# A new hand-placed order and new PSUM banks for a Conformer block on one core

## The chip, the cores and the metric

The kernel runs on one core of a Trainium2 chip. A core has engines that run side by side, each through its own list of instructions in order: TensorE (PE in the profile) multiplies matrices, and its weight loads (PEld) are listed apart; VectorE (DVE), ScalarE (ACT) and GpSimd (POOL) work on elements; SyncE (SP) does no arithmetic here and issues DMA transfers. Engines wait for one another through semaphores. TensorE writes its results to PSUM, a memory of banks; the other operands lie in SBUF. Full inputs and outputs lie in the chip's main memory.

The metric is the device time of one execution in microseconds (us). The profile covers one execution and gives its span, from the first to the last instruction that it shows; the execution's own time is a little longer.

## The reference

`x` is 2 sequences of 4,000 tokens with 144 features, all in bf16. Abridged:

```python
h = _layernorm(x);  h = _silu(h @ w_ff1a) @ w_ff1b          # 144 -> 576 -> 144
x = x + 0.5 * h
h = _layernorm(x);  qkv = h @ w_qkv                          # 4 heads of 36
p = _softmax((q @ k.T) * Dh ** (-0.5));  att = p @ v         # 4000 x 4000 per head
x = x + att @ w_o
h = _layernorm(x);  h = h @ w_pw1;  h = a * _sigmoid(b)      # 144 -> 2 x 144
c = sum(hp[:, i:i + T, :] * dw[i] for i in range(5))         # 5 taps along the tokens
x = x + _silu(c) @ w_pw2
h = _layernorm(x);  h = _silu(h @ w_ff2a) @ w_ff2b
x = x + 0.5 * h
return _layernorm(x)
```

The attention dominates: for 2 sequences and 4 heads, 4,000 × 4,000 scores, each with an exponential.

## The kernel before

**Tiles and stages.** The 8,000 tokens are cut into 16 chunks of 500 (numbers 0 to 15, eight to a sequence), and a chunk into 4 blocks of 125 rows. Each chunk goes through the first feed-forward, then queries, keys and values, then attention over its whole sequence, then the gated convolution, the second feed-forward and the last layernorm. The chunks' stages overlap: while one chunk is in attention, the one behind it is prepared and earlier ones are finished.

**Attention.** Keys are taken 64 at a time, 62 such tiles and one of 32 a chunk. For a tile TensorE makes the score products (`scores`, line 1770: `PS<-QT,KT`); their exponential goes to ScalarE (818 activations `PT<-PS`) or, for 190 tiles, to VectorE, which makes it from integer operations (`dve_tile`, line 1811); TensorE then multiplies it with the values (`PS<-PT,VA`, for the short tile `PS<-PT,VL`) and adds up in banks 6 and 7. All other products use banks 0 to 5.

**The rest.** In the feed-forward (`ff`, line 1240; `ff_part`, line 1258, for half a chunk) the first product is `PS<-XT,WA`, its last 64 columns are `PS<-XT,WE`, the activation gives `HT`, and the second product is `PS<-WB,HT`. While exponentials are being made, SiLU is made from tanh, which stands in the same table of functions (`TH` on ScalarE, then `HT` on VectorE); behind the last exponential ScalarE loads the table for SiLU (line 2102), and `HT` comes straight from ScalarE. The convolution is `PS<-U,DG`, products with diagonal matrices. A residual addition writes `X` on VectorE. The layernorm (`ln`, line 1109) takes statistics on VectorE (`ST`), a variance and a power on GpSimd (`RS<-RS,NHALF`), and then the normalised rows `XN` on GpSimd, or at both ends of the program on VectorE or ScalarE. For the last layernorm `store` (line 1661) writes `XN` to the output; `put` (line 1655) issues the transfer on SyncE's queue or, at the end of the program, on ScalarE's. The first and the last chunks go in two halves; the others in one.

**What sets the order.** The program is first recorded, not emitted: each call of `op` (line 177) notes an instruction and what it depends on, and a scheduler (`Sched`, line 509) picks with modelled costs which thread records next. That gives every engine a list of blocks (instructions that stay together). Then `R.reorder(ORDER)` (line 281, called on line 2115) permutes the blocks of each engine. A table, `ORDER` (line 38), has a string for each of the five engines; each character is one block's shift:

```python
codes, shift = [ALPHABET.index(c) for c in table[e]], []
...
shift.append(c - 45)
...
at[i + shift[i]] = blk
```

`P` has code 45 and leaves a block where it is; the next letters put it later, the ones before it earlier; `~` opens a longer shift of two further characters. A second table, `PLACES` (line 111), names with one digit the PSUM bank (0 to 5) of each of 1,724 tiles in the order in which they were recorded (`place`, line 257). For a new order the dependencies between tiles of one bank are made anew, `finish` (line 365) works out which semaphores each instruction waits for, and `replay` (line 409) emits each engine's list. All instructions are emitted on line 419, so the profile has them all under L419 and they are told apart by their tiles; the waits for the output's transfers at the end are on line 425.

Of the kernel before, what the change touches and what calls it, by code (L numbers as in the profile page):

```python
# [39 lines left out]
        "PPPPPPPPQOPPPPROQNPPQRPQLPPRPVPSPNIZMWOMVVL~OVKLJ~OOJJNSNLMMMNPNPKSOOJ[JZKMXNKOG]NJHEKNNNE_MMMadMJLL"  # L40
        "mTLI?LJLEMZPbJNJMGrLLLLkfJKKKKKWKNNVJMKgBJJJ[QddGGMIFKEcQKLJFKNKKNNKPUMOMWTMYVIRLLISKOLPQQRPRPJQUNPQ"
        "OQKPPPPPYOOOOYNNNOMhTNLVXLMIMOSXKILOKN`NNRRNHQOXROMQOTKOUQQQTQUS]PT[`P2ALQXDMKILMNTQLSKNRNUN_PMMNOWN"
        "]NNOOSKPRPDIOQOY__MWNNN]NHMNQCGMQJNWNORTOMRRTLTPNSOBOP^UNNQMMTLNPTLLTMNOWNOOOXNOPLOPNQQMTTNNNNRSO]OQ"
        "OPPGPNROMQQLPPQOPVOcNNNNPMTNNOM]]LNNKMNPWOPNJUOOCOOXOOYZOMKcLLWXJKKSWKHKKVJNNKNORPNPQOQOSOOVNOYZMMMM"
        "NNOMPXPKOOVQMNPVOPHPYMNOQNNPN[]^LMM]MKWKKKLJKLVLP`LN_NLNOMOQNKMRMNLPPPQOS[P[MOPISOKNQMIPRPSPLQNPWORO"
        "QQKLVOQRN[QQQQJFPPPPKQQSPRKQQLPPPQVPPQOPUUOOPNCXORRNYVSSNG[MPUZPPAOKAOMUNNPVOLTUOL]KLNRPMMSNNNNdZNQM"
        "MMNNQMSLLTYMOMSHVKUO]JJ`RKTNQKMFLNQNW[]NLPHLNQNRMNFPPPS]OOLOOPPSLNNNQOSOPN`SNOMNO_PMMNOMOOLPNPYVL^[Q"
        "LNKKFMQM[TLMOOQWNQVQMKYNRNXNO8NRMMNYOOQNN^OOOQOIOSP[OPRPZGOOPN]YMNNNO<VNNKMNOYPNOOOTQM]MVJSMMRMKSPUM"
        "HOPNSOOOSOPNTPNOOROOQVNOPNO^RPQMVOHNQNLPRPJPXOOPNPNOOPXXNNNOOOWNIOOOORUOPKOSNROTXKOW[KOKLN[RZIMOIKNN"
# [20 lines left out]
    "act": (  # L70
        "PPPPPPPPPPPPPRTNNOOPPQOPPPPPPXPNOSNNNNPPPPPPQRSOLOQZQORKRSLLOQQJPPPPQQNQOPPPPPPPPPQQQMPPPPPPPPPPPPRO"
        "OPQOPQQNPPPPPPPPPPPPPPPPPPPPPPPPPPPPPPPPPPPPPPPPPPPPPPPPPPPPPPPPPPPPPQOPRORNSNOOPPPPPPPPPQOPPPPPPPPP"
        "QOPPPPPPPPPPPQOPPPPPPPPPPPPQOPPPPPPPPPPPRPNPQOPPPPPRPNPPPPPPPPPPPPPPPPPPPPPPPPPPPPPPPPPPPPPPPPPPQOQQ"
        "NPPPPPPPPPPPPPPPPPPPPPPPPPPPPPPPPPPPPPPPPPPPPPPPPPPPPPPPPPPPPPPPPPPPPQOPPPPPPPPPPPPPPQOPPQOPPPPPPPPP"
        "PQOPPPPPPPPPPPPPPPPPPPPPPPPPPPROOPQOPPPPPPPPPPPPPPPPPPPQOPPPPQOPPPPPPPPPPPPPPPPPTOOPQQLPPPPPPPPPPPPP"
        "PPPPPQOPPQOPPPPPPPQOPPPPPPPPPPQOPPQOPPPPPQQQQLQQNPPPPPPQOPPPPPPPPPPPPPPPQOPPPQOPPPPPPPPPPPPPPPPPPPPQ"
        "OPPPPPPPTOPNOROOPPPPPPPPPPPPPPPQOPQOPPPPPPPPPPQOPPPPPPPPPPPQOPPPPPPPPPPPPPPPPQOPPPPPPPPPPQOPPPPPPPPP"
        "PPPRPNPPPPPPPPPQOPPPPPPPPPPPPPPPPPPPPPQRNOPPQQNPPPPPPPQQNPPPPPPPPPPPPPPPPPQOQOPPQOPPPPPPPPPPQOQOPPPP"
        "PPPQOQOPPPPPPPPPPPPPPPPPPPPPPPPPPPPQQNPPPPPPPPPPPPPPPPPPPPQOPPPPPPPPPPPPPPROOPPPPPPPPPPPPPPPPPPPPPQQ"
        "NPPPPQOPPPPPPPQQNPPPPPPPPPQOPPPPPPPPPPPPQOPPPPPPPPPPPPPPPPPPPPPPPPPPPPPPPPPPPPPPPPPPPPPPQOPPPPPPPPPP"  # L80
        "PPPPPPPPPPPPPPPPPPPPPPPPPPPPPPPPPQOSPNRNOQOUQNPMOPPPRORNQNPPPPPPQOROQQMPPPPPPQOPPPWORNNNOO"
    ),
# [2064 lines left out]
```

## Time and profile before

| what | value |
|---|---|
| three runs, median (lowest to highest) | 879.97 us (879.73 to 881.92) |
| the profiled execution | 880.01 us |
| its span in the profile | 878.1 us |
| instructions in the span | 27,043 |

The span and the execution's own time differ by 1.91 us, which lies around the span. In the profile's rows a group of instructions is written as engine, operation, output tile `<-` input tiles, sizes (partitions × elements, type) and a count; buffer numbers are left out, so `PS` is any PSUM tile. In a timeline the first two columns are the start and the length in us, and a bracket at the end gives the engine's idle time before and what ended it. A row of waits gives the total in us, the number and the longest.

### The profile page before, as it was taken

Reading aid. Unit: us, or ns where it says so; the run is one execution under the profiler, and the core shown is the slowest. Engines: PE = TensorE matmul, PEld = TensorE weight load, DVE = VectorE, ACT = ScalarE, POOL = GpSimd, SP = SyncE. Lnnn points to the kernel's source line nnn. Section 1 sums busy time; section 2 is a strip of 40 time slices with the busy share of each in tenths; the row PEclk is TensorE's granted clock in tenths of the full one; section 3 lists DMA queues with packets and bytes.
Section 4 is the critical chain, followed back from the end, with each engine's and each line's share of the span. In section 5 each row is a group of like instructions: output and inputs, shape, how many; then the busy total and the mean of one; then the engine's idle time right before and its main releaser. Section 6 shows DMA issues by size and latency. Waiting matters only on the chain.

```text
span 878.1 us, 27043 instructions
## 1 busy us (share of the span) xinstructions
PE 846.0 (96%) x11419; PEld 385.3 (44%) x11419; DVE 824.1 (94%) x1821; ACT 849.8 (97%) x1098; POOL 293.9 (33%) x573
## 2 busy tenths in 40 slices
PE   8999999999999999999999999999999999999996
PEld 6544443444444434443444444344434433443465
DVE  8978999999999999999989999899999999999987
ACT  6799999999999999999999999999999999999985
POOL 6650441241425332161323426223420116013434
PEclk9999999999999999999999999999999999999999
DMA  3221101211121020212001120100210011001111
GB/s 99 52 52 35 29 16 39 56 29 38 36 51 39 16 58 3 44 24 51 16 5 34 28 45 16 39 23 14 50 24 22 16 31 21 21 12 37 30 24 35
DMA packets 114353, 28.82 MB, mean 33 GB/s; under 512 B 101090, under 2 KB 114230, under 8 KB 114230
## 3 DMA queue, kind: packets, MB, share of 16 engines
q1 hardware_dynamic: 112646, 26.39, 13.8%
q8 instruction: 90, 1.47, 0.7%
q10 hardware_dynamic: 1584, 0.69, 0.3%
q14 instruction: 33, 0.27, 0.1%
HBM read 13.44 MB, written 13.61 MB: 31 GB/s over the span
## 4 chain that ended last, share of the span: by engine, by line
ACT 49%; PE 29%; DVE 16%; POOL 3%; DMA 1%; issue 1%; SPq 0%; ACTq 0%; POOLq 0%; DVEq 0%
ACT PT L419 45%; PE PS L419 29%; DVE PT L419 7%; ACT TH L419 4%; DVE ST L419 2%; POOL XN L419 2%; DVE HT L419 2%; POOL RS L419 2%; DVE XN L419 1%; DVE X L419 1%; DVE QT L419 1%; DMA X<-in_x_dram 0%; DMA XT<-rows 0%; DMA WE<-in_w_ff1a_dram 0%; DVE KT L419 0%
## 5 line engine op out<-in xcount | busy, mean ns | idle before, releaser
L419 ACT ACTIVATE PT<-PS 128x1000 bf16<-128x1000 f32 (+1 forms) x818 | 750.2, 1054 | 3.2 <-PE PS L419 2.0
L419 PE MATMUL PS<-QT,KT 64*64 64x500 bf16 x3968 | 420.0, 384 | 15.4 <-ACT PT L419 8.7
L419 PE MATMUL PS<-PT,VA 64*37 64x500 bf16 x4728 | 403.1, 372 | 0.7 <-DVE QT L419 0.4
L419 DVE TENSOR_SCALAR PT<-PS 128x500 int16<-128x500 f32 x380 | 251.0, 669 | 6.9 <-PE PS L419 5.5
L419 PEld LDWEIGHTS PS<-QT,KT 64*64 64x64 bf16 x3968 | 124.6, 104 | 236.5 <-ACT PT L419 132.0
L419 POOL TENSOR_SCALAR RS<-ST 125x4 f32<-125x4 f32 x130 | 39.8, 306 | 484.3 <-DVE ST L419 478.0
L419 PEld LDWEIGHTS PS<-PT,VA 64*37 64x37 bf16 x4728 | 142.8, 96 | 89.8 <-issue 13.3
L419 DVE TENSOR_SCALAR PT<-PT 128x1000 uint16<-128x1000 uint16 x380 | 152.7, 417 | 2.2 <-PE PS L419 1.0
L419 POOL TENSOR_SCALAR XN<-X,RS 125x144 bf16<-125x144 bf16 x260 | 146.8, 594 | 8.3
L419 DVE TENSOR_TENSOR PT<-PT 128x1000 bf16<-128x1000 bf16 x190 | 127.8, 675 | 1.1
L419 ACT ACTIVATE TH<-PS 128x500 bf16<-128x500 f32 (+3 forms) x194 | 101.7, 543 | 5.2 <-PE PS L419 4.3
L419 POOL TENSOR_TENSOR RS<-RS,NHALF 125x4 f32<-125x4 f32 (+1 forms) x93 | 91.9, 992 | 34.2 <-DVE RS L419 28.8
L419 DVE SCALAR_TENSOR_TENSOR HT<-TH,PS 128x500 bf16<-128x500 bf16 (+1 forms) x135 | 80.9, 615 | 9.3 <-ACT TH L419 8.6
L419 PE MATMUL PS<-XT,WA 80*128 80x500 bf16 (+5 forms) x288 | 74.5, 365 | 4.0 <-DVE XT L419 1.1
L419 DVE BATCH_NORM_STATS2 ST<-X 125x6 f32<-125x288 bf16 x160 | 65.7, 448 | 1.0 <-DMA X<-in_x_dram 0.8
L419 DVE SCALAR_TENSOR_TENSOR X<-PS,X 125x288 bf16<-125x288 f32 (+1 forms) x128 | 57.0, 450 | 6.5 <-PE PS L419 5.2
L419 PE MATMUL PS<-WB,HT 128*125 128x144 bf16 (+1 forms) x640 | 52.5, 230 | 0.8 <-ACT HT L419 0.5
L419 PEld LDWEIGHTS PS<-WB,HT 128*125 128x125 bf16 (+1 forms) x640 | 44.2, 136 | 14.5 <-issue 3.9
L419 PEld LDWEIGHTS PS<-XT,WA 128*128 128x128 bf16 (+1 forms) x288 | 21.3, 98 | 38.2 <-issue 9.4
L419 DVE STREAM_TRANSPOSE XN<-XN 128x320 f32<-128x320 f32 x54 | 27.2, 503 | 3.0 <-POOL XN L419 2.1
L419 PE MATMUL PS<-U,DG 128*128 128x250 bf16 (+6 forms) x204 | 29.3, 265 | 0.1
L419 POOL COPY U<-U 128x2 bf16<-128x2 bf16 (+1 forms) x54 | 10.0, 221 | 51.2 <-DVE U L419 51.2
(95 smaller groups left out, 519.2 us busy)
## 6 DMA issues: line engine op xcount, KB each, us to landing
rows<-XN SPq DMA_DIRECT2D x216, 40.0 KB, 2.0
XT<-rows SPq DMA_DIRECT2D x56, 128.0 KB, 2.1
rows<-AN SPq DMA_DIRECT2D x60, 40.0 KB, 2.0
X<-in_x_dram SPq DMA_DIRECT2D x15, 140.6 KB
XTQ<-rows SPq DMA_DIRECT2D x26, 70.3 KB
out_dram<-XN SPq DMA_DIRECT2D x13, 140.6 KB
XT<-rows SPq DMA_DIRECT2D x56, 16.0 KB, 1.9
out_dram<-XN SPq DMA_DIRECT2D x3, 70.3 KB
```

Of the source, the lines that this page charges most:

```text
L419: ins = getattr(eng, o.name)(*o.a, **o.k)
```

## The change

Only the two tables are changed. The instructions are the same 27,043 and each stays on its engine; every `cost`, function and size is as before. Waits, counted over the program, are 4,738 where they were 4,734. How many instructions get another place in their engine's list:

| engine | 0–60 us | 60 us to about 843 | from there on |
|---|---|---|---|
| TensorE | 215 of 613 | 6,522 of 10,487 | 319 of 319 |
| ScalarE | 17 of 88 | 56 of 957 | 51 of 61 |
| VectorE | 74 of 152 | 610 of 1,567 | 96 of 102 |
| GpSimd | 18 of 90 | 296 of 463 | 10 of 16 |
| SyncE | 0 of 66 | 131 of 389 | 4 of 11 |

Of the 1,724 tiles 109 get another bank: 15 of the first 120, 13 of those from 120 to 1,500, and 81 behind. In the diff, cut to the first and last rows of each engine and the last of the banks, the long rows of `P` on ScalarE show how little its exponentials move, and the last rows show that the end is arranged anew on all engines:

```diff
 ORDER = {
     "pe": (
-        "PPPPPPPPQOPPPPROQNPPQRPQLPPRPVPSPNIZMWOMVVL~OVKLJ~OOJJNSNLMMMNPNPKSOOJ[JZKMXNKOG]NJHEKNNNE_MMMadMJLL"
+        "PPPPPPPPQOPPPPPRPNPPQRROLPQRNWPSPNJ[MUOLTVL~OSLPI~OTIJNTNLMMMMPNPKSOPJ^JZJMYNKPGQNKHEKOOOC`NNNd`MKLL"
...
-        "NNNP^[NOMNNQMMOLNN]PNOOR[OPKQN_ZLNESMOOKHOM[NPPLPNOOPPMQSTMNPQQQQRSQRRTCQVNGRNOMTTTMMNUPPQHNQSPMYVTQ"
-        "KLLSSOIJPSSPTMKORNOQOPPPPPPSORNSMRNRRRNQQRPFRPQQQQQQRPFQO"
+        "MKNO[XMJNNQSLSGM^Q^QOPPP`ROMPM<BNQVMOLOMVPPTJOSZPLPSOPNPRRNUR>SPRLQ[SPROSdOAHPNKRRRZKKSJMM]kNbIQHMMO"
+        "MFMMPtKLnLMKMNJNLNNPNOOPNESOLNKQLSMKMQLPUQTHWLSMOTUULMNDRMO"
     "act": (
...
-        "NPPPPQOPPPPPPQQNPPPPPPPQOPPPPPPPPPPQOQPPPPPPPPPPPPPPPPPPPPPPPPPPPQOPPPPPPPPPPPPPPPPPPPPPPPQOPPPPPPPP"
-        "PPPPPPPPPPPPPPPPPPPPPPPPPPPQOSPNRNOQOUQNPMOPPPRORNQPPPPPQOROQQMPPPPPQOPPPWORNNNOO"
+        "NPPPPQOPPPPPPQQNPPPPPPPQOPPPPPPPPPPQOPQQNPPPQOPPPPPPPPPPPPPPPPPPPQOPPPPPPPPPPPPPPPPPPPPPPPQOPPPPPPPP"
+        "PPPPPPPPPPPPPPPQOPQOPPPPPPPPPPPVLPNSOYbZJKMNLMNLMNNQNPMOPQRPMSOOTNSNNNPPSNTMSLNWSORRILLQO"
     "dve": (
...
-        "QNPQQSPTQNPHPPROOQSNPQULPNOORROQRPJPPSOOORO]SOSNPRWQQXPTRERGRRTTUXRTRSBSSSSSSSSAT@S&NNPPPPPPPPPPQO"
+        "RLSQHRPSQOQFQZPMYNNaMNPivIJJNPJLLNwKLMKOLOKOKPNOPPQRRSNKR@M@OOXOO_OMORCNSTTWTWWCSHWAFGKUUMTLLMSPKO"
     "pool": (
...
-        "OVOOPNOQNPPPRPQM"
+        "TMOOQNPPQOPPPPQOQOPQQNQO"
     "sp": (
...
-        "WOVNNNNOMPPSORNQMPPPPSOOOPPWOQNNOOOPPPPQSNOOPPQQN"
+        "UOXNNNNPNOOVOSNOMNPPPROOPPPSOOOPPPPPPPPVVNNNNOQQKPPPPQOQO"
 PLACES = (
...
-    "0412041201412042041204024012412140214021401241205042304231514236404512412361021452243051351241353250"
-    "213024014452502542036410"
+    "0412040211412042040214024012412140134003423141203043503521015426305324423064214302103012310534200534"
+    "254421231352001535456524"
 )
```

The strings alone do not tell which instruction moves, since a shift counts from the place that the scheduler gave a block. At the program's end the new order comes to this: three pairs of `PS<-XT,WA` of chunk 11 go from ahead of the last `PS<-PT,VL` to behind it, and a pair `PS<-U,DG` goes ahead of it; chunk 11's `TH`, `HT` and residuals come 5 to 52 places later on ScalarE, VectorE and TensorE; chunks 14 and 15 come some 3 to 6 places sooner; of the last three groups of `PS<-WB,HT` the order was chunk 15's first half, chunk 15's second half, chunk 14's second half, and is now chunk 15's second half, chunk 14's second half, chunk 15's first half. The last two stores are now that of chunk 15's first half, on SyncE's queue, and that of chunk 14's second half, on ScalarE's.

More of the change, by code (lines that the diff above doesn't have):

```diff
@@ L45 @@
[L45 to L49, printed above, removed]
@@ new lines @@
+        "mRLI@LJKEMbXmJMILH`KKKKijIJJJJJWJLLWLMIhAJJJ[Pd^GHQIGIJbQKLJFKTLJLNLPVMOMPPTXTISMMJSLPMPPYPPRPKPTKNR"
+        "OQKPPPQOYOOOOUNNNOMfUNQWPMJJNPT^LJMPVO`OOHFNIQOXQOMQNSMOUQQQSQSW]OW^^O5BSN_GGHLIMMPRKQNLRNTN]VNLMNXM"
+        "]MOPNSJPRPCJOQOYZ_N`NNN]NHMNRBGMQJNVIOTXPLSPPJTQNSOCOPX[NNVMMOLLWSKLRLMNXOOOOZNNOMOPNPPMTUNNNNQTM]PQ"
+        "MPRINNRPMQQKPPQOPPPcOOOOPNTNNOM]YLNNKMNQVSPKKUOPCOOUOO]SMNL]MNX[LLLMWLILLWKNQKNORPMPQOQOTOPNOPYZNNNN"
+        "NNOMPVPKUOWQMMRUNQETXNINSMNNN]]_MMM_MKVKKKLJLJVLVcLMXJLLMNNVNLMPMOLOPPPPSSO[LPPKUOMNPNLPRPSPLQNTWPNL"
@@ new lines @@
+        "QQLMRPQSL[QQQQKIPPPPKPQSPRLQQLPPPPVPPPPPWUOOPNDXPRROYVSSND[MPUXPP@OKAOMROOQ[PMTOMN[MMNRPLLTNNNNhYNPM"
+        "MNNNSMSLLTYMOMQGUKTKSKKaSKPNSKPMMOQNZW[NLPHKNRMNROFPPPSZOOLOOPPWLNNPNOTNOO_RMNNPN_PMMNOMOPLPNPYWL^XQ"
+        "LPLLFHSMU[MMOOQXNRWRMK]OJOdOO8ORNNJTOOJNN[OOOQNIOOT[OPRP[HOOPN]XMNNNN=RNNSJNOXSNNNNTROXLWIVMNLNLSPUO"
+        "IOPNWOPNOOPNTPNOOROOQUNOPNOcRPQLUOJNPNLOQNNORNNPUORNNNY_NNNOMNOOLOOOORUOPKORNQNS^TNVTJNLIQ]YTINOGJMN"
+        "bMMN`NNVMNLMM`LMKMMWLPSXLMMPZU]CHOLJQ^SJKWNIQXILLSLLRLSLTNNOYNXNNOMNNNRRO_bOPNPZDLMMOMNJTQKMTISSMMMQ"
@@ new lines @@
+        "QNZOPNSO_XPbOHJ`GLLLLaOKKKMMMMRLM^MXMMPLLdMMMMNWMNPXLLMN^KMMMMR]MMTYMMNLRFNS`LINQNNT]WNLJLLNLYLRM[LL"
+        "QgLLLNVMMMMYVLLLYWMRMNWTNDDENXXOL]MMM]SMJ[[MKNE]LOLLSNYVBPNKTMDMNQQRR]NJOOOPX[NNJULLLMSSKUKLP^_LMTMM"
+        "MMMMNNOMQNPPWOYOQUNLPMWNEOXNNZNOKNOQOKROQQRPI]TRNNNPQOQUEOLPNPPPPPPPPPPQVQOTOOSHM^NVRNOMOQHROOJQQNbS"
+        "gMMSOOKNOOOOWSMALdPJMIQNPPTRPGMKOOPPMVOOOPROYKP`MN_SLLL_bKILLLNLJLOSKMMMVQM^aSJLLLM]MROLLYHKNLWL^lKK"
+        "LQKMKaMVLNLXLOVKKNNOJW?JNNOYOM]OMNNNNNOXNNNPQLNR^MNO^NNNNNXQLNPJO]UQO]JCPMOPIMPPPKPgOPNOOOQNVMUNLNNU"
@@ new lines @@
+        "VINO[LMVPNOBNOMOQOQOQOUOOOSOVORP]MGNPPMRWNNYTNPKQRZWBMPY]OOBKNOOENOOORPRROSbOQGROKPMQRRRNKQOGSPNOQOZ"
+        "OOOOOOOOOXNOPNQNTRLMW]OOTOHOMJOOP]MOOR[NLPUMNIMMNOPPPVOSOMNNR_NPMPNRSMXOKKOMS[LMQLNOUNPNRNJQOPSOOOPQ"
+        "SSYOZLOOQQNRCOVHQNWMNPULNQMMQRSOWOPWHPNOUZWNLWELLNL]LMOQNN]WMOLLQLNQJNSNOOSTPQLLPPQOYQOPPPQOPGPRXNNT"
+        "NNNNNPWOPXOYNORHNJPLOPaPNOTOMVOMTQNTW]O^WUEOMOOIP:?PNPPPPPPPPPQRPQLPPSOVRMOTKOVLNPNRNQVQKNVOMQMVMQMP"
+        "MQRTLQMNQSNVOMOOPNXSOMNPMUNN[OO[KQN[TTMN_KQKC]NNZ@MMM[LLLLSMKXSLLZLLOMNPNVNUMMNVRMKNOSUbYKLNPPWKOVEK"
@@ new lines @@
+        "LNLMSMOXPROQQMXORPQTLOOR>OQOPPPQWROLPMW^MMR]LMKLNR[LLLOQJMWNXMMMNW]LLMMVRLLLMNQQLSUOMSMNSWORNOPUQNPW"
+        "BTMOPSSTINWOPSEPTLSOORROFS^NNSMNXZLLRMKM[LIOMdQULLLMULLSMMMMRWMPYKKYOQKKSLZMQJQKQW]WNKHLXTKKMJNRKRMZ"
+        "NPVaLOZKNLSOPJcDOJO_SIRMJLTQJMKWRTIQIJS]KQ^LOUJM]MKWTZJOIKYJCNPJPLOVNScMNRVLUHLSTKLT[JGYKPXKIYMOSLHN"
+        "HWNNYbMRLYTTPJHKEJZRLNKMPPMOSNOVPMOSSNSKPSJPN]`aMNLMMMOMKMMMPSLRNJPPYOROMRUOMJROLR]NNSZMMMPLSLWLLLPN"
+        "UOMT]XMKLMTTUMWYLJGOPNBRNYPLQNPMTOMTaPMTPM]TMMPMMYWPLL_KULQLLXNPNPXSL,]KKOMQOQKW^NKQLLXLQ[KMWJSLLNPM"
@@ L81 @@
[L81 removed]
+        "PPPPPQOPPPPPPPPPPPPPPPPPPPPPPPROOPQOPPPPPPPPPPPPPPPPPPPPPPPPPQOPPPPPPPPPPPPPPPPPSOOQQQLPPPPPPPPPPPPP"
+        "PPPPPQOPPQOPPPPPPPQOPPPPPPPPPPQOPPQOPPPPQQQQQKQQNPPPPPPPPPPPPPPPPPPPPPPPQOPPPQOPPPPPPPPPPPPPPPPPPPPQ"
+        "OPPPPPPPTOOOOROOPPPPPPPPPPPPPPPQOPQOPPPPPPPPPPQOPPPPPPPPPPPQOPPPPPPPPPPQOPPPPPPQOPPPPPPPPPPPPPPPPPPP"
+        "PPPRPNQOPPPPPPPQOPPPPPPPPPPPPPPPPPPPPPPROOPRPQMPPPPPPPQQNPPPPPPPPQOPPPPPPPPPQOPPQOPPPPPPPPPPQOQOPPPP"
@@ new lines @@
+        "JFJTILLDWEEMJMBMKLLFLLLLLLLLLMMMNSPROLPPRPNPQOROQQQLQOQQNPQQNPPQOQOQOQOPPPQOROOPRPQVQOYPNOPQOQOVWRVQ"
+        "UU:KNHQQRSSPSQRRSZSSSSLRVQUI=OO-PROQNPRPRSLPRPQJQOPPPPPPUPQbSMSOTOQEUQFNJNQMRPQQQQHQOQQNQORPNROQNRPN"
+        "QOQQNQQNPPRORPMPPPROQRMQRPQQQWPPPQQSSLOQSQOQQRPRP5PPXPPPPPPPHROOPPPPPPPPPQOPPPPPPPPPROSNPNQOPPQQTMOO"
+        "RNQQMRPRPQQQQHPPPPSPPTRPNQHQOPQOTPPPLQOROOPPPQVNOOOOOUOPSSVNLUPPMEOQOPPQOPPQQRPQKPROOPPPPQOPPPPPPPQO"
+        "PRPQQQKQOPXOQSQTKTLVMRNUNQNAOPPXOPNPNPPRPQQjPPPUOOOANNPNOOOOSNNNNOOOOPPPPPPPPRPQQRRJQMSOOQNQOPSOPNPP"
@@ new lines @@
+        "PYPNOOVOOLOVORPNPGSOOOSPPMPQOQOPSPPQQQJRPRMRNQQMPPPPPPPPPPQOPUOQNSOROJTOOOOQQNROQTTPKMNPPPPPPPPPPQSP"
+        "PLQOPPPRPNPQOPPPPPPPQOPPPQOPPUOOOOOVOPNPNOPPPPPTQNRSQRTIUIWMTOKLRMMQOQOPPPPPQOPPPRORNOPQQNPQORORNOSO"
+        "OOPPPPQOPQOQQNQOROOPQOPPPRPNPPPQOPPPPPTOOOOPQOPSPNOPQQRSOKQNPPSPNQNPQOPPSOSQSLLOPPQOQOQOTOOOOPPTOOOO"
+        "PPROQQRPRPQHPPPPPPPPPPPPQOQOPUPNOPNRSNTMNSNNVNUPMOLNPROOROVNPPMPQMPPPPPPSQNQMPVOQOQOVQQUGOKNOPPPPPQO"
+        "PPUOOOOOPQQRPQQQIQTPMOOPPPPPPPPQTNOPSMPNPRTOWLNNPNOOPROQNROOPPPPRRNQMQQNPSOOOPQOROQRMRRTRPRIRPHRPNPR"
```

77 lines of the change are left out of this document (22 added, 55 removed).

## Prediction

> **What bounds the kernel now.** I read the page first, then busy time by stretch, the waits, and the timeline of both ends.
>
> ```profile
> span 878.1 us, 27043 instructions
> PE 846.0 (96%) x11419; PEld 385.3 (44%) x11419; DVE 824.1 (94%) x1821; ACT 849.8 (97%) x1098; POOL 293.9 (33%) x573
> ACT 49%; PE 29%; DVE 16%; POOL 3%; DMA 1%; issue 1%; SPq 0%; ACTq 0%; POOLq 0%; DVEq 0%
> L419 ACT ACTIVATE PT<-PS 128x1000 bf16<-128x1000 f32 (+1 forms) x818 | 750.2, 1054 | 3.2 <-PE PS L419 2.0
> ```
>
> Three engines are 94 to 97% busy, and the chain that ended last runs through ScalarE, TensorE and VectorE in turn. An average over the span does not tell which one a stage lacks, so here is the busy time of four stretches (columns: stretch, length, then each engine's busy time):
>
> ```profile
> core 0: us, PE busy (x) PEld busy (x) DVE busy (x) ACT busy (x) POOL busy (x), PEclk, DMA share, GB/s
> 0.00:60.00 60.00, 54.43 (x612) 33.09 (x613) 51.30 (x150) 47.15 (x82) 41.87 (x94) 1.00 0.31 70
> 60.00:842.00 782.00, 762.92 (x10481) 328.22 (x10478) 742.88 (x1567) 778.62 (x958) 239.92 (x462) 1.00 0.14 30
> 842.00:871.50 29.50, 28.66 (x333) 23.94 (x331) 27.99 (x97) 22.29 (x56) 10.33 (x17) 1.00 0.10 26
> 871.50:878.10 6.60, 0.01 (x1) 0.00 (x0) 1.90 (x9) 1.70 (x4) 1.82 (x3) 0.85 0.18 53
> ```
>
> The front (to 60) has no full engine. In the middle, the attention, ScalarE is idle for 782.00 − 778.62 = 3.38 us: its exponentials are the bound. From 842 to 871.5 it is TensorE, idle for 29.50 − 28.66 = 0.84 us. Behind it comes the chain of the last block: residual, layernorm, store.
>
> **The change part by part.** No instruction is added, removed, changed or given to another engine: the sums of busy time stay, and only idle time can move. I counted moves and positions from the two programs' own instruction orders. The sum is made against the profiled execution, 880.01 us (the span and 1.91 around it); the median of the three runs is 879.97, 0.04 below.
>
> *Front, 0 to 60.* 17 of 88 ScalarE, 74 of 152 VectorE, 215 of 613 TensorE and 18 of 90 GpSimd instructions change place, SyncE's none.
>
> ```profile
> 30.00:35.00 5.00, 4.60 (x37) 2.67 (x36) 4.96 (x14) 2.80 (x5) 3.57 (x9) 1.00 0.39 89
> 35.00:40.00 5.00, 4.68 (x69) 3.36 (x67) 5.00 (x14) 3.82 (x9) 2.01 (x3) 1.00 0.11 33
> 40.00:45.00 5.00, 4.90 (x34) 2.18 (x33) 5.00 (x13) 4.67 (x10) 3.94 (x8) 1.00 0.19 33
> 39.80 0.51 DVE L419 STREAM_TRANSPOSE XN<-XN 128x320 f32<-128x320 f32 x1
> ```
>
> From 30 to 45 VectorE is full, so there only the order of its work counts. The largest move is the transpose of the last row: it goes five places back and lets what feeds TensorE and ScalarE start 0.51 earlier, while the transpose's own readers wait longer. I take −0.2, less than half of it. As bounds I take one such transpose each way, ±0.5.
>
> *Middle, 60 to 842.* The order of the exponentials on ScalarE is nearly the same, but TensorE's moves a great deal (5,790 of 9,631), as do 521 of 1,440 on VectorE, 240 of 407 on GpSimd and 116 of 361 on SyncE's queue. What counts is where the score products, which the exponentials wait for, stand among the rest. Summing TensorE's work ahead of each of the 818: 417 unchanged, 196 earlier by 0.2 us or more, 135 later, these by 0.30 us in the mean and in 78 runs of neighbours.
>
> ```profile
> PEld PS L419 <- ACT PT L419: 142.9, 401, 0.9
> ACT PT L419 <- PE PS L419: 1.1, 4, 0.4
> ```
>
> These are waits between 60 and 842 (total, times, longest). TensorE's weight loads waited 401 times for ScalarE to release a score bank, 142.9 / 401 = 0.36 us in the mean; ScalarE waited for scores only 4 times. So a score product usually comes as early as its bank permits, and one that moves 0.30 back eats a slack of 0.36. That slack is the cover of this part, and I cost it at 0. The most it can gain is the 3.38 us of idle time; if no run of neighbours were covered, it would lose 78 × 0.30 = 23.4. The row of 142.9 is the nearer one: it is 401 cases against 4. Bank changes (13 of the middle's tiles, among 109 of all 1,724) can only alter which release is waited for, so they lie in the same bounds. SyncE's moved transfers sit behind waits of its queue and its readers come many microseconds later; they, and GpSimd with 239.92 busy of 782, I cost at 0 too.
>
> *End of the attention, around 842.*
>
> ```profile
> 838.83 0.28 ACT L419 ACTIVATE TH<-PS 64x125 bf16<-64x125 f32 x1
> 839.13 2.38 ACT L419 ACTIVATE PT<-PS 128x1000 bf16<-128x1000 f32 x3
> 841.74 0.62 PE L419 MATMUL PS<-XT,WA 128*128 128x500 bf16 x2
> 842.20 0.38 PE L419 MATMUL PS<-U,DG 128*128 128x375 bf16 x2
> 843.04 0.42 PE L419 MATMUL PS<-PT,VL 64*101 64x500 bf16 x2
> 843.39 0.60 PE L419 MATMUL PS<-U,DG 128*128 128x250 bf16 x4
> 843.83 0.62 PE L419 MATMUL PS<-XT,WA 128*128 128x500 bf16 x2
> ```
>
> The small tanh at 838.83 moves behind the last exponential, which then ends 0.28 earlier than 839.13 + 2.38 = 841.51. Three pairs of XT,WA products (chunk 11's second feed-forward) move behind the last attention product, PT,VL; one pair of U,DG (convolution) moves ahead of it. A pair XT,WA takes 842.20 − 841.74 = 0.46, four U,DG take 843.83 − 843.39 = 0.44, so a pair 0.22. Thus 3 × 0.46 − 0.22 = 1.16 us of TensorE's work leaves the way of the last attention product, which is over about 1.16 sooner. But the same 1.16 is then still to be done, in a stretch that TensorE bounds: net 0. It would be worth something only for what stands idle behind it, which the next part counts.
>
> *The stretch TensorE bounds, 842 to 871.5.* All 319 of its instructions from 843 on are rearranged, so are 96 of VectorE's 102, 51 of ScalarE's 61 and 10 of GpSimd's 16, and 81 tiles have new banks. The work is the same, so at most the 0.84 of idle can be gained; TensorE waited there for these two:
>
> ```profile
> PE PS L419 <- DMA XT<-rows: 0.5, 1, 0.5
> PE PS L419 <- ACT HT L419: 0.3, 1, 0.3
> 867.50 0.38 PE L419 MATMUL PS<-XT,WE 128*128 128x250 bf16 x2
> 868.64 0.84 PE L419 MATMUL PS<-WB,HT 128*125 128x144 bf16 x10
> 870.67 0.84 PE L419 MATMUL PS<-WB,HT 128*125 128x144 bf16 x10 [0.34 <-ACT HT L419]
> ```
>
> The last three groups of WB,HT were chunk 15's first half (868.64), chunk 15's second half, chunk 14's second half (870.67). Now chunk 15's first half comes last, directly behind chunk 14's second half. Its joint is XT,WE, then the activation HT, then WB,HT; 867.50 to 868.64 shows 1.14 us for it with other products between. With chunk 14's group (0.84) as filler, TensorE waits 1.14 − 0.84 = 0.30 at this joint, and I add 0.14 for a similar one before it: 0.44 of the 0.84 stays, and the sum takes −0.4. Ends: −0.84 if every wait goes; +2 if the two joints stand open whole (2 × 1.14 − 0.3).
>
> *Behind the last group.*
>
> ```profile
> 871.72 0.45 DVE L419 SCALAR_TENSOR_TENSOR X<-PS,X 125x288 bf16<-125x288 f32 x1
> 872.21 0.46 DVE L419 BATCH_NORM_STATS2 ST<-X 125x6 f32<-125x288 bf16 x1
> 872.28 1.70 ACT L419 ACTIVATE XN<-X,RS 125x144 bf16<-125x144 bf16 x4 [1.66 <-DVE RS L419]
> 872.70 0.17 DVE L419 TENSOR_SCALAR RS<-ST 125x2 f32<-125x2 f32 x1
> 872.95 0.69 POOL L419 TENSOR_TENSOR RS<-RS,NHALF 125x2 f32<-125x2 f32 x1 [0.32 <-DVE RS L419]
> 873.21 1.02 SPq L419 DMA_DIRECT2D out_dram<-XN  x2
> 873.68 0.54 DVE L419 TENSOR_SCALAR XN<-X,ST,RS 125x144 bf16<-125x144 bf16 x2 [0.75 <-POOL RS L419]
> 874.00 0.77 ACTq L419 DMA_DIRECT2D out_dram<-XN  x2
> ```
>
> Before, counted from 870.67: residual +1.05, statistics +1.54, variance +2.03, GpSimd's power +2.28 to +2.97, VectorE's XN +3.01 to +3.55, its store on ScalarE's queue, the end at 878.1, +7.43. After, the last group's chunk (15) has this chain to GpSimd's power, but chunk 14's second half follows it on VectorE and GpSimd, one power later: +2.97 to +3.66. ScalarE then normalises chunk 15 (a quarter of 1.70, 0.43 each, two blocks) and SyncE stores it at about +4.15. VectorE normalises chunk 14's half last: +3.71 to +4.25, behind the second power by the same 0.05 as above. So the last store's data come 4.25 − 3.55 = 0.70 later after the last group. Ahead of it one store fewer is still in flight, since the half of chunk 15 that was stored beside it goes out some 2 us earlier; but chunk 15's first half starts only 0.2 before it. I take +0.7; ends 0 (the two powers do not meet) and +1.4 (twice).
>
> Sum: 880.01 − 0.2 + 0 + 0 − 0.4 + 0.7 = 880.1.
>
> **The rivals.** *Scores too late for ScalarE (slower).* Some of the 78 runs of neighbours are not covered, since the slack of 0.36 is a mean, and the longest wait for scores was already 0.4. Price 0.30 a run; with the rest of the sum it passes the bound of 0.3% (2.64 us, about what a measurement of this kernel can tell from no change) from nine uncovered runs on. A fifth, 16, gives 4.7 and 884.8. For it: TensorE has 762.92 of 782.00 busy, too little to catch up quickly. Against: the 196 products that come earlier, and 4 waits in 818.
>
> *The front shrinks (faster).* In the first 60 us TensorE is idle for 60 − 54.43 = 5.57 us, VectorE 8.70, ScalarE 12.85. If the rearranged front brings the first exponentials forward by half of TensorE's idle, 2.8, all that follows moves with it, since the middle has work for a full ScalarE: 880.1 + 0.2 − 2.8 = 877.5, and 877.1 with the tail's other 0.4. Against: VectorE is full from 30 to 45, and the loads keep their order.
>
> *The stores decide the end (no change that counts).*
>
> ```profile
> 874.00:875.00 1.00, 0.00 (x0) 0.00 (x0) 0.22 (x1) 0.00 (x0) 0.00 (x0) 1.00 0.26 71
> 875.00:876.00 1.00, 0.00 (x0) 0.00 (x0) 0.00 (x0) 0.00 (x0) 0.00 (x0) 1.00 0.32 91
> SPq L425 <- DMA out_dram<-XN: 2.9, 3, 1.3
> ```
>
> While the stores drain, the DMA share is 0.32: about 5 of 16 engines work. The final waits are three, 2.9 us together, nearly 1.0 each. If the last stores go out one behind the other on the same five and two instead of three are left, the end comes 1.0 sooner rather than 0.7 later: 880.01 − 0.2 − 0.4 − 1.0 = 878.4. The Trainium skill's page "DMA: Bandwidth & Descriptors", section "Why a DMA increments its semaphore by 16 and not by 1", says as much: a transfer issued from SyncE or ScalarE uses the largest number of engines up to 16 that divides its slowest dimension, always the lowest-numbered; 125 rows give five. The trace's 0.32 agrees. By that rule the time is this rival's 878.4, by my rows 880.1. I prefer the rows because the last store's data are late whatever drains ahead.
>
> **How the numbers follow.** Forecast or the stores' rival, within 0.3% (877.4 to 882.6): 0.34 + 0.12 = 0.46; own range 878.4 to 882.1, from the sums of the front's and tail's smaller ends. Scores too late, slower: 0.30, because 135 products come later and the loss has a long end while the gain ends at 3.38. A shorter front or middle, faster: 0.24. The range takes in 3.5 us of gain (877.1 as above, less 0.5 from the middle: 876.6) and the fifth uncovered (884.8); a tenth stays out on each side.
>
> **What would show it.** Right: ScalarE's idle in 60 to 842 stays near 3.4 and its waits for scores few; the first 60 us hold the same busy times within 0.5; last group of WB,HT starts within 0.8 of 870.67 and is chunk 15's; from there to the last store's XN 4.25 instead of 3.55; two instead of three final waits for stores. Wrong: "ACT PT" waits for "PE PS" in the dozens (first rival); ScalarE's busy time in the first 60 us grown by 2 or more (second); the end nearer than 7.4 to the last group (third). The sum fails first in the middle, where 0 stands for an interval of −3.4 to +23.4.

## The result, and the profile after

The changed kernel takes 881.91 us (median of 19 runs, 881.46 to 882.75), the kernel before 879.94 (19 runs, 879.32 to 881.92). The ratio is 1.0021, with a 95% interval of 1.0014 to 1.0028: it is slower by about 2 us, 0.22%. The forecast was 880.1, within 0.3% either way, in a range of 876.6 to 884.8. The side within 0.3% held; the sum was 1.8 too low, and it was not the summed mechanism that kept the time inside (see below). The profiled execution took 881.79 us.

The page after and its busy time by stretch, in the same columns as before:

```profile
span 879.9 us, 27058 instructions
ACT 36%; DVE 26%; PE 26%; POOL 9%; issue 2%; DMA 1%; SPq 0%; POOLq 0%; DVEq 0%
0.00:60.00 60.00, 54.14 (x607) 32.91 (x607) 51.59 (x149) 47.03 (x82) 41.13 (x93) 1.00 0.30 70
60.00:842.00 782.00, 762.26 (x10476) 324.69 (x10469) 743.98 (x1566) 777.48 (x955) 238.48 (x458) 1.00 0.14 30
842.00:871.50 29.50, 29.00 (x327) 23.89 (x328) 26.25 (x92) 23.80 (x58) 10.85 (x22) 1.00 0.10 26
871.50:879.90 8.40, 1.57 (x21) 1.27 (x19) 3.96 (x15) 2.59 (x6) 2.54 (x4) 0.76 0.20 58
```

ScalarE's idle time between 60 and 842 us grew from 3.38 to 782.00 − 777.48 = 4.52, and in the chain that ended last VectorE and GpSimd have 26% and 9% where they had 16% and 3%. That is the first pointer: work that leads to ScalarE now passes through those two.

Better than sums is the start of each exponential, the same one in both traces. The table gives how much later it starts than before; it was worked out from the two lists of instructions. Its starts are counted from the first arithmetic instruction, 0.24 us less than in the timelines. The list of ScalarE is nearly the same in both up to the 815th exponential (behind it the short one goes ahead of two others), so the column is the lag of the whole pipeline.

| exponential | start before, us | after minus before, us |
|---|---|---|
| 19th | 57.46 | −0.45 |
| 25th | 63.75 | +0.12 |
| 109th | 143.87 | +0.36 |
| 207th | 240.66 | +0.84 |
| 319th | 352.96 | +1.16 |
| 389th | 419.50 | +1.61 |
| 571st | 603.90 | +1.33 |
| 697th | 724.27 | +1.57 |
| 815th | 837.56 | +1.64 |

The lag comes in steps of 0.1 to 0.6 us at a few places and is flat in between for long stretches. The first step is between the 19th and the 25th. Here is that place in the timeline after, for GpSimd, VectorE, TensorE and ScalarE:

```profile
52.00 0.80 DVE L419 BATCH_NORM_STATS2 ST<-X 125x6 f32<-125x288 bf16 x2
52.89 0.20 POOL L419 TENSOR_SCALAR RS<-ST 125x4 f32<-125x4 f32 x1 [1.39 <-DVE ST L419]
54.62 2.32 POOL L419 TENSOR_SCALAR XN<-X,RS 125x144 bf16<-125x144 bf16 x4
56.97 0.51 DVE L419 STREAM_TRANSPOSE XN<-XN 128x320 f32<-128x320 f32 x1 [0.71 <-POOL XN L419]
57.41 0.96 DVE L419 SCALAR_TENSOR_TENSOR HT<-TH,PS 128x500 bf16<-128x500 bf16 x2
58.10 0.59 PE L419 MATMUL PS<-XTQ,WQ 72*128 72x500 bf16 x2 [0.62 <-DVE HT L419]
59.05 0.41 PE L419 MATMUL PS<-QT,KT 64*64 64x500 bf16 x4
59.50 1.00 ACT L419 ACTIVATE PT<-PS 128x1000 bf16<-128x1000 f32 x1 [0.35 <-PE PS L419]
```

And the same place before:

```profile
47.69 0.80 DVE L419 BATCH_NORM_STATS2 ST<-X 125x6 f32<-125x288 bf16 x2
51.21 0.19 POOL L419 TENSOR_SCALAR RS<-ST 125x4 f32<-125x4 f32 x1
54.75 0.51 POOL L419 TENSOR_SCALAR XN<-X,RS 125x144 bf16<-125x144 bf16 x1
55.95 1.26 DVE L419 SCALAR_TENSOR_TENSOR HT<-TH,PS 128x500 bf16<-128x500 bf16 x2 [0.48 <-ACT TH L419]
57.13 0.50 DVE L419 STREAM_TRANSPOSE XN<-XN 128x320 f32<-128x320 f32 x1
57.85 0.60 PE L419 MATMUL PS<-XTQ,WQ 72*128 72x500 bf16 x2
57.70 2.79 ACT L419 ACTIVATE PT<-PS 128x1000 bf16<-128x1000 f32 x3
```

Read it from the third row down. GpSimd's last normalised block XN is done at 54.75 + 0.51 = 55.26 before and at 54.62 + 2.32 = 56.94 after. The transpose of these rows, on VectorE, stood behind the two HT before and stands between them now. VectorE takes its list in order, so it stands idle for 0.71 us, with a ready HT queued behind. A projection on TensorE needs the bank that this HT releases and waits 0.62; the score product behind it in TensorE's list comes late; and ScalarE, at the end of the row, is idle for 0.35.

The first two rows tell why XN was late, and it was not GpSimd's own doing. From its first step for this block to its last XN GpSimd took as long as before (51.21 to 55.26, and 52.89 to 56.94: 4.05 us). It had stood idle for 1.39 us for the block's statistics ST, which moved seven places back in VectorE's list, from 47.69 to 52.00. So at this place VectorE's list has both ends of the trouble: the statistics later, the transpose that needs what GpSimd makes of them earlier.

The waits of VectorE for GpSimd's XN between 40 and 842 us, before and then after, show that this is no single case (the last row is ScalarE's waits for scores after, where the prediction's row has 1.1 us and 4):

```profile
DVE XN L419 <- POOL XN L419: 1.5, 4, 0.5
```

```profile
DVE XN L419 <- POOL XN L419: 5.0, 10, 1.2
ACT PT L419 <- PE PS L419: 2.0, 7, 0.4
```

Four waits of 1.5 us became ten of 5.0. The longest is here (VectorE, after), at one of the steps, and a further one is at 835 us:

```profile
400.48 0.51 DVE L419 STREAM_TRANSPOSE XN<-XN 128x320 f32<-128x320 f32 x1 [1.19 <-POOL XN L419]
835.42 0.51 DVE L419 STREAM_TRANSPOSE XN<-XN 128x320 f32<-128x320 f32 x1 [0.62 <-POOL XN L419]
```

At the end, the last attention product, the last group's second feed-forward (its weight loads), the last XN, the last store and the final waits are now:

```profile
843.68 0.42 PE L419 MATMUL PS<-PT,VL 64*101 64x500 bf16 x2
872.33 0.69 PEld L419 LDWEIGHTS PS<-WB,HT 128*125 128x125 bf16 x10 [0.25 <-ACT HT L419]
875.84 0.54 DVE L419 TENSOR_SCALAR XN<-X,ST,RS 125x144 bf16<-125x144 bf16 x2 [0.51 <-POOL RS L419]
876.42 0.26 ACTq L419 DMA_DIRECT2D out_dram<-XN  x1
SPq L425 <- DMA out_dram<-XN: 2.3, 2, 1.7
```

Against before the last attention product is 0.64 later (843.04 to 843.68), from there to the last group 28.65 us instead of 27.63, and from the last group to the end 7.57 instead of 7.43: 0.64 + 1.02 + 0.14 = 1.80, the difference of the spans. Busy times between the last attention product and the last group, before and then after:

```profile
843.04:870.67 27.63, 26.79 (x316) 22.97 (x312) 26.14 (x93) 21.26 (x55) 9.80 (x13) 1.00 0.10 24
```

```profile
843.68:872.33 28.65, 28.06 (x319) 23.59 (x315) 26.34 (x93) 22.94 (x57) 10.27 (x19) 1.00 0.10 25
```

### The profile page after: what moved, and what is told of

The parts are those of the page before. It is cut to its first block, busy times and chain, and to the rows that moved or that the text cites. A ratio compares the mean times of both kernels' runs of the same rounds, so it can differ in the third digit from the quotient of the medians.

```text
span 879.9 us, 27058 instructions
## 1 busy us (share of the span) xinstructions
PE 847.0 (96%) x11419; PEld 382.8 (44%) x11419; DVE 825.8 (94%) x1821; ACT 850.9 (97%) x1098; POOL 293.0 (33%) x573
## 4 chain that ended last, share of the span: by engine, by line
ACT 36%; DVE 26%; PE 26%; POOL 9%; issue 2%; DMA 1%; SPq 0%; POOLq 0%; DVEq 0%
ACT PT L419 33%; PE PS L419 26%; DVE PT L419 13%; POOL XN L419 5%; POOL RS L419 4%; DVE ST L419 3%; ACT TH L419 3%; DVE HT L419 2%; DVE XN L419 2%; DVE X L419 2%; DVE QT L419 1%; DVE AN L419 1%; DMA X<-in_x_dram 0%; DVE KT L419 0%; DVE SW L419 0%
## 5 line engine op out<-in xcount | busy, mean ns | idle before, releaser
L419 POOL TENSOR_SCALAR RS<-ST 125x4 f32<-125x4 f32 x130 | 35.3, 272 | 506.4 <-DVE ST L419 500.2
L419 DVE TENSOR_SCALAR PT<-PT 128x1000 uint16<-128x1000 uint16 x380 | 154.7, 421 | 1.6 <-PE PS L419 0.2
L419 POOL TENSOR_SCALAR XN<-X,RS 125x144 bf16<-125x144 bf16 x260 | 149.7, 605 | 14.3 <-DMA out_dram<-XN 6.1
L419 POOL TENSOR_TENSOR RS<-RS,NHALF 125x4 f32<-125x4 f32 (+2 forms) x93 | 91.5, 987 | 32.8 <-DVE RS L419 27.2
L419 PE MATMUL PS<-XT,WA 128*128 128x500 bf16 (+5 forms) x288 | 74.7, 364 | 4.9 <-DVE XT L419 1.3
L419 DVE SCALAR_TENSOR_TENSOR X<-PS,X 125x288 bf16<-125x288 f32 x128 | 57.3, 451 | 6.8 <-PE PS L419 6.0
L419 PE MATMUL PS<-U,DG 128*128 128x250 bf16 (+7 forms) x204 | 29.1, 264 | 0.1
L419 PE MATMUL PS<-IDF,QT 128*125 128x128 f32 x128 | 22.9, 302 | 0.3 <-DVE QT L419 0.2
```

The costliest lines, as they stand in the source:

```text
L419: ins = getattr(eng, o.name)(*o.a, **o.k)
```

## The experiments

Times that the expectations name inside a kernel are counted from the first arithmetic instruction and are 0.24 us smaller than those of the timeline. Since all orders are strings of shifts, the edits are shown as moves of blocks in an engine's list.

### Which stretch

Four kernels take the new order and the new banks in one stretch alone, on all engines, with the order of before elsewhere. The stretches were cut at places that the same blocks precede in both orders.

```diff
 lists of all five engines, kernel before
-order and banks of before in [0, 60) / [60, 436) / [436, 748) / [748, end)
+order and banks of the change in that one stretch
```

> The kernel before with the new order and banks only for what stood in its first 60 us. Theory A (the loss is a sum of small waits of ScalarE in the first half of the middle, +1.2 us, and of the tail, +0.7): between -0.4 and +0.3 us against before, since the 21st exponential ended at 60.27 in the changed kernel and 60.25 before. Rival B (all of the loss is behind the attention): 0. Rival C (the loss is set in the front, by other banks and transposes, and only shows later): +1 us or more.

> The kernel before with the new order and banks only from 60 to 436 us. Theory A: +1.0 to +1.6 us, since the exponentials of the changed kernel fall behind from +0.02 at 60 to +1.53 at 436 us, in steps of 0.15 to 0.5. Rival B: under +0.3 us, because the lag of ScalarE is taken up by slack before the end. Rival C: 0.

> The kernel before with the new order and banks only from 436 to 748 us. Theory A: -0.4 to 0 us, since the lag of the exponentials goes from +1.53 to about +1.3 us in this stretch. Rivals B and C: 0.

> The kernel before with the new order and banks only from 748 us to the end. Theory A: +0.4 to +1.0 us: the last exponential not later than before, the last WB,HT group about 0.4 later, and from its start to the last store's XN 4.05 us instead of 3.55. Rival B: +1.7 to +2.2 us. Rival C: 0 or a gain.

| stretch | median, us (before 879.89) | ratio, 95% interval |
|---|---|---|
| 0 to 60 | 880.90 | 1.0013 (1.0004 to 1.0021) |
| 60 to 436 | 881.34 | 1.0016 (1.0007 to 1.0025) |
| 436 to 748 | 879.78 | 1.0002 (0.9993 to 1.0011) |
| 748 to the end | 880.66 | 1.0007 (0.9998 to 1.0016) |

Theory B falls: the stretch from 60 to 436, far from the end, costs 1.45 us by itself, so the lag of ScalarE does reach the end. The front cost 1.01, more than theory A allowed and as much as rival C asked for; but C had 0 for the stretch from 60 to 436, so it falls as the whole account and holds for a part. The front's trace shows the transpose's wait again (longest 0.7 us) and the step between the 19th exponential (−0.04) and the 25th (+0.75). The other three came out as theory A had them. The four differences add up to 3.1 us, more than the 1.97 of the whole change; with intervals of some 0.75 us on each that decides nothing, and two of them are cut through at 60 us, where the front's gain of 0.45 is lost.

### What makes the steps

The steps coincide with the transposes that wait. The next kernel moves nothing but nine transposes, and the one after it tries the other reading, that TensorE's list puts the scores too late:

```diff
 VectorE, changed kernel, around 57 us (likewise at eight more places, 1 to 3 blocks later)
-STREAM_TRANSPOSE XN
 HT<-TH,PS
 HT<-TH,PS
+STREAM_TRANSPOSE XN
```

```diff
 TensorE, changed kernel, around 58 us (likewise at 104 and 369 us)
+score products PS<-QT,KT
 projection PS<-XTQ,WQ
 projection PS<-XTQ,WK
-score products PS<-QT,KT
```

> The changed kernel with nine row transposes (STREAM_TRANSPOSE XN<-XN) moved one to three places later in VectorE's list, behind work that is ready. Theory D: in the changed kernel VectorE waits in its list for GpSimd's XN at nine of these places before 840 us (0.28 to 1.19 us each, 4.8 in all; four places and 1.5 us before), what is queued behind comes late, TensorE waits for it, and ScalarE at last: then this kernel is 0.8 to 1.5 us faster than the changed one, 880.4 to 881.1. Rival E (TensorE's own order puts the score products too late; VectorE's waits are covered): within 0.3 of the changed kernel's 881.9.

> The changed kernel with three blocks of score products moved on TensorE ahead of the projection that waits for VectorE, at 58.8, 103.7 and 369.1 us. ScalarE was idle behind these three for 0.36, 0.06 and 0.21 us and lost 0.5, 0.2 and 0.2 us against before. Theories D and E both: 0.5 to 0.9 us faster than the changed kernel, 881.0 to 881.4, since the scores' banks were free 0.6 to 0.8 us before. If the lag is caused by the banks or by something that follows later: within 0.3 of 881.9.

With the nine transposes moved the kernel takes 879.90 us (11 runs, 879.42 to 880.37), a ratio of 0.9999 to before (0.9991 to 1.0008). All of the 2 us is gone, more than expected, by moves on VectorE alone; TensorE's list, ScalarE's list and the banks are those of the changed kernel. The same place in its trace:

```profile
55.54 1.26 DVE L419 SCALAR_TENSOR_TENSOR HT<-TH,PS 128x500 bf16<-128x500 bf16 x2 [0.39 <-ACT TH L419]
57.68 0.50 DVE L419 STREAM_TRANSPOSE XN<-XN 128x320 f32<-128x320 f32 x1
60.61 0.51 DVE L419 STREAM_TRANSPOSE XN<-XN 128x320 f32<-128x320 f32 x1 [0.84 <-POOL XN L419]
57.37 0.60 PE L419 MATMUL PS<-XTQ,WQ 72*128 72x500 bf16 x2
57.21 3.69 ACT L419 ACTIVATE PT<-PS 128x1000 bf16<-128x1000 f32 x4
```

VectorE's wait, TensorE's wait and ScalarE's gap at 57 us are gone together, and four exponentials follow one another without a gap. XN is as late as in the changed kernel, though: the next transpose, at 60.61, now waits 0.84 us where it waited 0.22, and 0.28 us is still lost up to the 25th exponential. Comparing the exponentials of this kernel with those of the changed one gives each wait's price: 0.29 us at 57, 0.24 at 237, 0.44 at 317, 0.30 for the four between 354 and 401, 0.13 at 688, 0.42 at 835; 1.82 in all, of 4.78 us of waiting. The 0.13 is no larger than a step by which two traces with the same lists differ (see the end); the others are.

Moving the score products made things worse: 882.86 us, where 881.0 to 881.4 was expected, a ratio of 1.0038 (1.0024 to 1.0051). ScalarE and TensorE at 57 us:

```profile
57.71 2.79 ACT L419 ACTIVATE PT<-PS 128x1000 bf16<-128x1000 f32 x3
61.31 1.00 ACT L419 ACTIVATE PT<-PS 128x1000 bf16<-128x1000 f32 x1 [0.81 <-PE PS L419]
58.76 0.41 PE L419 MATMUL PS<-QT,KT 64*64 64x500 bf16 x4 [0.83 <-ACT PT L419]
60.46 0.26 PE L419 MATMUL PS<-WQKV,XTQ 72*64 72x72 bf16 x4 [0.35 <-DVE QT L419]
```

The exponential whose scores were moved has no gap any more; the next one waits 0.81. The projection now starts behind the score products, its copy QT on VectorE comes later, and the next score product is queued behind a product that waits for that copy. The late engine was VectorE; another order on TensorE only passes its lateness on. This was a miss for theories D and E both, which had expected a gain: I had looked at one exponential and not at who is queued behind the block that was moved back.

### One wait, other waits, more waits

```diff
 e9_one: changed kernel, only the transpose at 57 us moved behind both HT
 e10_before4: kernel before, its four waiting transposes, two blocks later each
 e11_early: kernel before, seven transposes 2 to 6 blocks earlier
 e12_tail: new order from 748 us on, with the transpose at 835 us three blocks later
```

> The changed kernel with a single transpose moved, the one for which VectorE waited 0.71 us at 56.73, two places later. Theory D, with each wait paying for itself: 0.3 to 0.5 us faster than the changed kernel's 881.9, and the 41st exponential that much earlier. Rival F (the nine waits act together, or the later ones absorb an early gain): within 0.2 of 881.9.

> The kernel before with the four transposes for which VectorE waits there (at 353.5, 550.6, 615.6 and 734.6 us, 1.53 us in all) moved two places later each. If every wait of VectorE for GpSimd costs about what it lasts: 0.8 to 1.5 us faster. Theory D with the cover (a wait costs only what ScalarE then stands idle, and ScalarE's longer idle times before lie elsewhere): within 0.3 of before.

> The kernel before with seven transposes moved two to six places earlier in VectorE's list, so that VectorE stands 0.6 to 1.2 us for GpSimd at each, about 6 us in all; no other order changed. Theory D: 1.0 to 3.0 us slower than before. If the loss of the changed kernel needs more than these waits (banks, TensorE's order): under 0.5 us slower.

> The kernel before with the changed order from 748 us on, and in it the transpose that waits at 835.2 moved three places later. Theory D: of the 0.8 us that the changed order of this stretch cost, 0.3 to 0.5 go, and 0.2 to 0.6 over before are left. If the 0.8 is all behind the attention (last groups, powers, stores): still 0.6 to 1.0.

One transpose alone: 881.37 us, 0.54 under the changed kernel's 881.91, with a ratio of 1.0005 to before (0.9996 to 1.0015). The two times were not taken side by side (before took 880.35 beside the one and 879.94 beside the other), so the trace has to bear the reading. In its trace the step from the 19th to the 25th exponential is 0.26 instead of 0.57 us, and from there on the two columns run parallel but for one step of 0.13 in this kernel's favour at 199 us, where the lists agree. An early gain is not eaten later: rival F falls.

Seven transposes moved earlier in the kernel before: 886.08 us, a ratio of 1.0060 (1.0045 to 1.0075), far more than the 1 to 3 us that were expected. VectorE's waits for XN between 40 and 842 us, ScalarE's for scores, and the worst place on TensorE and ScalarE:

```profile
DVE XN L419 <- POOL XN L419: 7.2, 11, 1.2
ACT PT L419 <- PE PS L419: 5.2, 10, 1.2
689.51 0.40 PE L419 MATMUL PS<-QT,KT 64*64 64x500 bf16 x2 [1.09 <-DVE PT L419]
690.37 1.00 ACT L419 ACTIVATE PT<-PS 128x1000 bf16<-128x1000 f32 x1 [1.04 <-PE PS L419]
691.68 1.00 ACT L419 ACTIVATE PT<-PS 128x1000 bf16<-128x1000 f32 x1 [0.30 <-PE PS L419]
692.93 1.00 ACT L419 ACTIVATE PT<-PS 128x1000 bf16<-128x1000 f32 x1 [0.25 <-PE PS L419]
```

The waits are 7.2 − 1.5 = 5.7 us more. The exponentials are 0.46 late at the 17th, ahead of the first of the seven waits, and 7.20 at the last: 6.7 us for them. No TensorE order and no bank was changed here, so such waits are sufficient. The worst place is 688 us, with 2.7 us for one wait of 1.17: VectorE comes late with the `PT` that releases the scores' bank, TensorE waits 1.09 for it, and three gaps of ScalarE follow one another.

The four waits that the kernel before has of its own: 879.70 us against 880.35 of before on the same chip, a ratio of 0.9997 (0.9985 to 1.0009). The time cannot tell this from no change. The trace can: this execution started its exponentials 1.95 us late, because the first transfers came late (VectorE waited 2.1 us for `X` where it had waited 0.8), and its lag then fell to 1.17, by 0.25, 0.28 and 0.26 near 551, 616 and 735 us, where three of the four transposes were moved; the fourth gave nothing. So the ratio is what theory D with the cover had, but the reason given there (ScalarE's idle times lie elsewhere) does not fit the trace. The prices were hidden in gaps that hardly show, as told below.

The last stretch with its one transpose repaired: 880.11 us, 0.24 below the kernel before on the same chip, where without the repair it was 0.77 above; the ratio to before is 0.9994 (0.9985 to 1.0004). So less is left than the 0.2 to 0.6 that were expected. Between the two traces the exponentials step by 0.42 at the 813th, behind the repaired transpose, and the spans differ by 0.5 (878.7 and 878.2). So the transpose at 835 us accounts for about half of the 0.8; nothing is left that the end behind the attention would have to explain, but the intervals, some 0.8 us each way, cannot settle the rest.

### A better mixture, and the stores

```diff
 e7_best: kernel before
+order and banks of the change in [0, 748), its eight transposes there moved as above
```

```diff
 e8_stores: kernel before, behind R.reorder(ORDER)
+    lost = [o for o in R.ops if o.q in ("o16", "o17", "o18")]
+    R.ops = [o for o in R.ops if o not in lost]
```

> The changed order to 748 us with its eight transposes of that stretch moved as in the first kernel, and the order of before from 748 us on. The front of the changed kernel is 0.45 us ahead at 56 us and loses it at 59; the stretch from 436 to 748 gains 0.26. Theory D: 879.2 to 880.2 us, the old tail's 0.8 and the waits saved. Rival E: 881.0 to 881.3, the changed kernel less the tail's 0.8.

> The kernel before without three of its last four output stores (chunk 15's first half, its second half and the single row), so that these rows are not written; everything else as before. If stores queue one behind the other at the end, the last one ends 1 to 2.5 us sooner: 877.4 to 878.9. If the last store's own time sets the end, within 0.3 of before.

The mixture takes 879.87 us, ratio 0.9999 (0.9990 to 1.0008): within theory D's bounds, but no gain. No version here is shown to beat the kernel before.

Without three of the last four stores the kernel takes 878.83 us, ratio 0.9988 (0.9979 to 0.9997), 1.13 less. Its last store and the final waits:

```profile
873.49 0.54 DVE L419 TENSOR_SCALAR XN<-X,ST,RS 125x144 bf16<-125x144 bf16 x2 [0.75 <-POOL RS L419]
874.07 0.28 ACTq L419 DMA_DIRECT2D out_dram<-XN  x1
```

That is the small end of what was expected. From the last XN, done at 874.03, to the end of the span at 876.7 it is 2.67 us; with all four stores before it was 878.1 − 874.22 = 3.88. Of these 1.21 us some 0.2 are the issue: before, the last store stands behind another one on ScalarE's queue, and its issue ends 0.55 behind XN (the prediction's row at 874.00), here 0.32 behind. The other 1.0 is what three stores, one with a single row, delay the last one while they are in flight: 0.3 to 0.5 a store, not the 1.0 that the prediction read from the final waits. That a store in flight delays another is in line with the rule in the Trainium skill's page "DMA: Bandwidth & Descriptors", section "Why a DMA increments its semaphore by 16 and not by 1", by which stores of 125 rows share the same five engines.

## Why the prediction was right or wrong

**Range and side.** They held in part by luck. The 881.91 lies 0.2 inside the prediction's own range of 878.4 to 882.1, whose upper end no sum in it gives, and the loss came from the middle, which the sum had at 0. The 0.3% is also more than a measurement of this kernel needs to tell a time from no change: the interval of the ratio is 0.07% each way.

**The bounds of the stages.** Right. ScalarE bounds the middle so strictly that a lag it gets at 57 us is there at 840.

**Front, −0.2.** The sign held to 57 us, where the 19th exponential starts 0.45 earlier. The step that failed is the reading of VectorE's order from 30 to 45 us, by one transpose that goes five places back and makes only its own readers wait. Just behind, statistics went seven places back (47.69 to 52.00) and the transpose that needs them one place ahead, to where its input is not ready; that cost 0.57 by the 25th exponential.

**Middle, 0.** Here most of the error lies: the lag goes from +0.12 to +1.64, 1.52 us. Two steps failed. The 521 moved instructions of VectorE are counted, but the cost of 0 is argued for TensorE, the banks, SyncE and GpSimd ("with 239.92 busy of 782"), not for them. That GpSimd has time is an argument from an average: its XN still came 1.7 us late at 57, since its input did, and VectorE's transposes stood where XN was not ready. And the cover was counted for TensorE's own moves only. The slack of 0.36 is what TensorE has against ScalarE; a block of VectorE that comes 0.7 late uses it up at once. What would have told it was not looked at: how long before its turn each transpose has its input (at 57 us before, XN was done at 55.26 and read at 57.13).

**Rival "scores too late".** Right in sign, wrong in its mechanism, and the time stayed inside the 2.64 us from which it counted. The 135 score products that moved back still stand there in the kernel with nine transposes moved, which is as fast as before. Nor did ScalarE's waits for scores come in the dozens: 7 instead of 4.

**End of the attention, 1.16 sooner.** Right in the main. The 815th exponential is 1.64 late and the last attention product 0.64: 1.00 gained, and given back behind it. Only 0.58 of it is TensorE's, since the last exponential ends at 842.73 where it was 841.51, 1.22 late; 0.42 was gained on ScalarE, where the small tanh now stands behind the last exponential and the short exponential ahead of two others.

**The stretch TensorE bounds.** The forecast was +1.16 for the work moved behind and −0.4 for the waits, +0.76; measured +1.02. In the rows of these stretches TensorE's idle time went from 27.63 − 26.79 = 0.84 to 28.65 − 28.06 = 0.59, 0.25 gained, and its busy time grew by 1.27: both terms are off by 0.1 to 0.2. The last group starts 1.66 us later than 870.67, more than the 0.8 that the prediction named as a sign of being right.

**Behind the last group, +0.7.** To the last XN it was 876.38 − 872.33 = 4.05 us, with 4.25 forecast and 3.55 before. To the end it was only +0.14. The term was too high mostly by the drain of the stores, 3.52 instead of 3.88 us: the stores' rival, with a third of the size that it was given; the final waits are two instead of three, as forecast. Front and tail together came to 0.28 where 0.1 was forecast, in part because their parts erred in opposite ways; the sum failed in the middle, as the prediction had named it.

**Rival "the front shrinks".** Half a microsecond of it was there, and was lost at 57 us.

## What to carry to other kernels

Where several engines with in-order lists work at over 90%, a change of order is priced by asking, for every block that waits for another engine, whether its input is there when its turn comes; what stands behind it in the list pays for the wait, and the price can arrive two engines further. Compare the starts of the same instruction on the bounding engine between two traces: a lag that comes in steps names the places, and each place can then be read in a few rows. Repair the engine that is late, not the one that is seen waiting, and follow a late input back to where it began: at 57 us the way led over GpSimd to VectorE's own statistics.

## What the runs showed that I had not expected

ScalarE's idle rows understate what a gap costs. An activation of 1000 columns lasts 1.00 us or a little more in the rows (1.05 in the mean), but four in a row take 3.69 (the row at 57.21 above), so they start about 0.9 apart, each beginning before the other's end. Here is an exponential behind a tanh in the kernel before, and the same two with the transpose moved (the four waits above):

```profile
552.14 0.30 ACT L419 ACTIVATE TH<-PS 80x125 bf16<-80x125 f32 x1
552.48 3.90 ACT L419 ACTIVATE PT<-PS 128x1000 bf16<-128x1000 f32 x4
```

```profile
554.09 0.31 ACT L419 ACTIVATE TH<-PS 80x125 bf16<-80x125 f32 x1
554.25 2.00 ACT L419 ACTIVATE PT<-PS 128x1000 bf16<-128x1000 f32 x2
```

Before, the exponential starts 0.04 behind the end of the activation ahead of it; with the transpose moved it starts 0.15 before that end. A gap shown as 0.04 cost 0.19.

Two executions whose lists agree keep the same distance within some 0.03 us over hundreds of microseconds, but not always: the kernel with the single transpose and the changed one differ by a step of 0.13 at 199 us, and the kernel without three stores and the one before by 0.07 at 618, with the same lists there. The largest differences enter in the first 20 us (0.04 to 2.9 us at the first exponential in these traces). So single traces can price steps of 0.2 us that the times of ten runs cannot; one of 0.1 they cannot.
